# A delta-rule attention and a routed MLP in one kernel: the first inverse moved to one engine, residual and block product in tiles of their own, pairs without padding, late steps routed one by one, and the first 256 places of expert 0 computed between the two stages

## The chip, the cores and the metric

The kernel runs on one core of one Trainium2 chip. The metric is the time of one execution on the device, in microseconds (us). A core has a tensor engine (PE; its weight loads are shown apart, as PEld), a vector engine (DVE), a scalar engine (ACT), a GpSimd engine (POOL) and a sync engine (SP) that issues transfers. Each works through its own queue of instructions in order, and semaphores make one wait for another.

## The reference

Two layers are chained. The first is a linear attention with the delta rule: for each of 4 batches and 8 heads a state of 48 x 48 is carried over 768 tokens. The second is a mixture of 8 experts over the 3072 tokens of width 384, each token going to the one expert with the highest logit.

```python
k_n = k / (np.linalg.norm(k, axis=-1, keepdims=True) + 1e-06)
for t in range(S):
    kt, vt, bt = (k_n[:, :, t], v[:, :, t], beta[:, :, t, None])
    y[:, :, t] = np.einsum('bhd,bhde->bhe', q[:, :, t], state)
    v_old = np.einsum('bhde,bhd->bhe', state, kt)
    state = state + bt[:, :, :, None] * np.einsum('bhd,bhe->bhde', kt, vt - v_old)
...
logits = x @ w_gate
expert_idx = np.argmax(logits, axis=1)
...
for e in range(E):
    h = np.maximum(x_sorted[lo:hi] @ w1[e], 0.0)
    y_sorted[lo:hi] = h @ w2[e]
return (gate_w[:, None] * y).astype(np.float32)
```

With this input the experts get 342 to 410 tokens each, expert 0 gets 401.

## The kernel before, in words

**Chunks and groups.** The 768 tokens are cut into 24 chunks of C = 32; step `c` handles chunk `c` for all 4 batches at once, one batch to each 32 partitions. Inside a chunk the recurrence is a triangular system, one 32 x 32 matrix for each batch and head. Four chunks form a group, `GS = 4`; the inverses of the 128 matrices of a group (4 steps, 8 heads, 4 batches) are made together on DVE by `invert(g)` (L267), one matrix to a partition: transposes in (L281), the norms of the keys by a few operations on 32 columns (L290 to L329), a scaling (L339), 30 pairs of a multiplication (L350) and an addition (L355), one pair to a row of the matrix, a scaling back, and transposes out (L362). The result is `ub`.

**Group 0 is made in another way.** For it `K = 2`: DVE inverts the two 16 x 16 diagonal blocks of each matrix side by side, with 14 pairs instead of 30, and `across` (L376) puts the corner in with matmuls: a product on PE (L384), its eviction on ACT (L389), a second product (L398) and an addition on DVE (L406), once for each of the four steps. These are `chores`, taken at fixed places of the steps.

**A step** (L445). On PE, in this order: the state times the keys is added to the scaled values, which `begin` put there (L439, L453), giving the residual in `pc[:, 0]`; ACT evicts it as `R` (L464); `logits` of an earlier chunk go to columns 384 on of `pc[:, 1]` (L558, evicted at L562); the block product `ub` times `R`, 32 matmuls of 32 x 32 (L473), goes to `pc[:, 1]`, and ACT evicts it as `Z` (L479); the state times the queries (L453); the product of keys and `Z`, added into the sums `acc` (L492), which ACT copies to `states` (L500); the transposes of the chunk before, `turn` (L538), into `pc[:, 0]`; the rest of the output (L511), evicted as `xg` (L521) and written to `xs` in memory. ACT also scales the values of the next chunk (L419). `pc` is one tile of two banks with one buffer, so all these share it.

**What sets the order.** The queues are written out by hand. The main loop (L697) runs a step, lets DVE work on inverses with `fill(4.0)`, runs the small routing work that is `urgent`, computes the scores of a later chunk (`score`, L525, L242), begins the next step, and runs `fill(2.8)`; the argument is a budget in us, which `fill` (L172) charges with 0.165 + 0.00104 n per operation of n elements, or 0.09 + 0.00104 n when it alternates between two inverses. `keep_scores` (L249) masks the scores into `gt` and `qk` with two operations (L260). At the start of a group the loop finishes that group's inverse first. Scores are computed 6 chunks ahead at the start (`FRONT`), and one more at steps 0, 5 and 8 (`EXTRA`). Where no scores are left, `heat` runs a matmul without a use (L431).

**Layouts.** Keys and queries come in pairs of heads: 48 rows of one head padded to 64, so that a pair has 128 rows. `kq` holds them, `wide_kq` holds them again with zeros where the other head is. The keys by token (`kt`) are padded to 64 columns a head.

**Routing** (L568). When the last chunk of a batch of `BATCHES` has its logits, DVE finds each token's expert, PE ranks the tokens of an expert (L605), DVE adds the counts so far (L618 to L631), and POOL writes the tokens' numbers to their places in `lists` by one indirect transfer for each chunk (L633); each waits for the one before. The gates are written beside `xs` (L650). The last batches are chunks 16 to 19, 20 to 22, and 23.

**Experts.** After step 23 (the seam) the lists are read back (L738, L742); for each expert POOL clears a tile and gathers the tokens' rows (L760, L762): three tiles of 128 places and one of 64. `expert` (L775) transposes them, multiplies with w1 (L790), applies the ReLU, multiplies with w2 (L806; the 64 places in another way, L820), scales with the gate and scatters to the output (L770). In fp32 each matmul shows as two entries in the trace. Weights of expert 0 come in pieces during steps 4 to 17; those of experts 1 and 2 are asked for in the seam (L132, L133), when the attention's memory is free.

Of the kernel before, what the change touches and what calls it, by code (L numbers as in the profile page):

```python
# [14 lines left out]
I32 = mybir.dt.int32  # L15
# [6 lines left out]
B, H, S, D = 4, 8, 768, 48  # L22
C = 32
# [17 lines left out]
FRONT = 6  # L41
EXTRA = (0, 5, 8)
LG = DM
RK = LG + E
LEAD = 10
BATCHES = [[0, 1, 2, 3], [4, 5, 6, 7], [8, 9, 10, 11], [12, 13, 14, 15],
           [16, 17, 18, 19], [20, 21, 22], [23]]


def _f32_consts():  # L50

# [11 lines left out]
    own = t // (C // 2) == w // (C // 2)  # L63
    kk = 1.0 * (t == w) - (t < w)
    k0 = 1.0 * (t == w) - ((t < w) & own) - (t // (C // 2) > w // (C // 2))
    return np.concatenate(
        [kk, k0, -1.0 * (t < w), rev, base, more, p < j, np.ones((128, 128))], axis=1
# [4 lines left out]
def kernel(  # L72
# [23 lines left out]
    nc.scalar.dma_start(out=cf[:, 0 : 3 * C], in_=src[:, 0 : 3 * C])  # L96
# [4 lines left out]
    def part(w):  # L101
# [4 lines left out]
    mask_g, mask_0, mask_q, rev, base, further, upper, ones = (  # L106
        part(w) for w in (C, C, C, E, E, E * MAXR, 128, 128)
# [37 lines left out]
    psS = att.enter_context(tc.tile_pool(name="psS", bufs=1, space=PSUM))  # L145
    psC = att.enter_context(tc.tile_pool(name="psC", bufs=1, space=PSUM))
    psQ = att.enter_context(tc.tile_pool(name="psQ", bufs=1, space=PSUM))
    psA = att.enter_context(tc.tile_pool(name="psA", bufs=1, space=PSUM))
    att.enter_context(tc.manual_schedule())
# [3 lines left out]
    states = persist.tile([128, B, NP, 2, D], FP32, name="states")  # L153
    acc = psS.tile([128, B, 512], FP32, name="acc")

    wide_kq = [persist.tile([128, 2, NP, 2, 128], FP32, name=f"wkq{i}") for i in range(3)]
    LW = E * LIST // 128
    empty = persist.tile([128, LW], I32, name="empty")
    warm = persist.tile([128, 512], FP32, name="warm")
    fdt = persist.tile([128, GS * H, C], FP32, name="fdt")  # L160

    kqs, kts, vts, qks, gts, ubs, norms, vss, xgs, lgs = ({} for _ in range(10))
# [3 lines left out]
    behind, later, soon, chores = deque(), deque(), deque(), deque()  # L166
    scored, front = [0], [None]
# [3 lines left out]

    def fill(us):  # L172


        while us > 0 and behind:
            n = next(behind[0], None)
            if n is None:
                behind.popleft()
                continue
            us -= (0.09 if len(behind) > 1 else 0.165) + 0.00104 * n  # L180
            if len(behind) > 1:
                behind[0], behind[1] = behind[1], behind[0]

    def chore():
        if chores:
            chores.popleft()()

    def urgent():

        for work_ in soon:  # L190
            for _ in work_:
                pass
        soon.clear()
        soon.extend(later)
        later.clear()
# [23 lines left out]
    def scores(c):  # L219

        if c >= NS:
            return None
# [697 lines left out]
```

## Time and profile before

| | |
|---|---|
| time, median of 3 runs | 668.01 us (664.99 to 671.21) |
| span of the profiled run | 670.4 us |
| PE, busy | 577.2 us, 86% |
| DVE, busy | 238.6 us, 36% |
| ACT, busy | 169.2 us, 25% |
| POOL, busy | 105.4 us, 16% |
| granted PE clock, mean | 0.923 |
| expert products L790, L806, L820 | 148.5, 125.1, 22.4 us |
| row operations L350 and L355 | 52.7 and 53.0 us |
| heating L431 | 43.8 us, 86 entries |

A line of the profile's groups or timeline gives the engine, the line of the kernel, the operation, output and inputs by name, the shape, and in brackets the idle time of the engine before it and what ended that. `x32` in a timeline is a run of 32 such instructions. Busy PE time is the sum of overlapping entries, so a busy PE need not be PE at its best. A busy share over the whole span mixes stages: the experts fill PE, the steps before them don't. In the strip of 40 slices each digit is a tenth of a slice of 16.8 us; the line PEclk shows the granted clock in tenths.

### The profile page before, as it was taken

Reading aid. Unit: us, or ns where it says so; the run is one execution under the profiler, and the core shown is the slowest. Engines: PE = TensorE matmul, PEld = TensorE weight load, DVE = VectorE, ACT = ScalarE, POOL = GpSimd, SP = SyncE. Lnnn points to the kernel's source line nnn. Section 1 sums busy time; section 2 is a strip of 40 time slices with the busy share of each in tenths; the row PEclk is TensorE's granted clock in tenths of the full one; section 3 lists DMA queues with packets and bytes.
Section 4 is the critical chain, followed back from the end, with each engine's and each line's share of the span. In section 5 each row is a group of like instructions: output and inputs, shape, how many; then the busy total and the mean of one; then the engine's idle time right before and its main releaser. Section 6 shows DMA issues by size and latency. Waiting matters only on the chain. (4 is left out here: it accounts for less than half of the span.)

```text
span 670.4 us, 18338 instructions
## 1 busy us (share of the span) xinstructions
PE 577.2 (86%) x8120; PEld 358.0 (53%) x8121; DVE 238.6 (36%) x773; ACT 169.2 (25%) x441; POOL 105.4 (16%) x111
## 2 busy tenths in 40 slices
PE   4777758847878988887979999999999999999991
PEld 3356646636656765665435555555555545555550
DVE  4825655789967968011111021111102020111100
ACT  0124325434545556552001010101001010101101
POOL 4000000110010101102240131402213140311011
PEclk9967679787989899888989999999999999999996
DMA  9933336655653334211075012423234342310000
GB/s 320 268 103 98 97 96 194 132 144 136 186 143 105 69 93 92 75 37 26 2 247 197 24 51 106 150 95 121 52 123 132 118 142 106 121 33 36 2 23 12
DMA packets 38882, 72.15 MB, mean 108 GB/s; under 512 B 10310, under 2 KB 25078, under 8 KB 38800
## 3 DMA queue, kind: packets, MB, share of 16 engines
q1 hardware_dynamic: 33072, 60.99, 30.7%
q0 software_dynamic: 4608, 9.47, 4.5%
q8 instruction: 64, 1.05, 0.7%
q10 hardware_dynamic: 1120, 0.50, 0.3%
q14 instruction: 18, 0.15, 0.1%
HBM read 62.16 MB, written 10.35 MB: 108 GB/s over the span
## 5 line engine op out<-in xcount | busy, mean ns | idle before, releaser
L790 PE MATMUL phe<-xTe,w1t 128*128 128x448 f32 x384 | 148.5, 547 | 0.0
L806 PE MATMUL pye<-w2t,hT 128*128 128x384 f32 x384 | 125.1, 486 | 0.0
L790 PEld LDWEIGHTS phe<-xTe,w1t 128*128 128x128 f32 x384 | 73.2, 192 | 70.1 <-issue 67.8
L806 PEld LDWEIGHTS pye<-w2t,hT 128*128 128x128 f32 x384 | 73.0, 190 | 51.7 <-issue 3.0
L633 POOL DMA_INDIRECT lists<-ids,ri x24 | 23.5, 979 | 291.7 <-DVE ut L355 140.9
L795 DVE TENSOR_SCALAR hT<-phe 128x448 f32<-128x448 f32 x32 | 20.0, 625 | 127.5 <-PE phe L790 127.5
L770 POOL DMA_INDIRECT out_dram<-y,rows x24 | 24.0, 1002 | 214.5 <-ACT y L815 181.1
L355 DVE TENSOR_TENSOR ut<-ut,tmp 128x58 f32<-128x58 f32 (+9 forms) x164 | 53.0, 323 | 4.8
L350 DVE TENSOR_TENSOR tmp<-ut 128x58 f32<-128x58 f32 (+9 forms) x164 | 52.7, 322 | 5.1
L799 ACT ACTIVATE hT<-phe 128x448 f32<-128x448 f32 x32 | 17.4, 543 | 144.6 <-PE phe L790 144.6
L419 ACT ACTIVATE vs<-vt,normt 128x48 f32<-128x48 f32 x192 | 47.8, 324 | 7.8 <-DVE normt L324 7.8
L473 PE MATMUL pc<-R,ub 32*32 32x48 f32 x1472 | 25.1, 222 | 24.0 <-DVE tmp L350 10.1
L500 ACT ACTIVATE states<-acc 48x768 f32<-48x768 f32 x46 | 37.0, 804 | 32.8 <-PE acc L492 28.7
L431 PE MATMUL pa<-warm,ident 128*128 128x512 f32 x86 | 43.8, 655 | 0.0
L785 DVE COPY xTe<-px 128x448 f32<-128x448 f32 x24 | 14.2, 614 | 80.7 <-PE px L781 80.7
L815 ACT ACTIVATE y<-pye,xin 128x384 f32<-128x384 f32 x16 | 9.3, 580 | 133.2 <-PE pye L806 133.2
L492 PE MATMUL acc<-Z,kt 32*128 32x96 f32 x736 | 33.3, 324 | 3.3 <-issue 3.3
L473 PEld LDWEIGHTS pc<-R,ub 32*32 32x32 f32 x1472 | 21.2, 119 | 26.9 <-issue 19.2
L558 PE MATMUL pc<-wg,xT 128*128 128x8 f32 x144 | 21.3, 268 | 13.9 <-ACT R L464 10.3
L492 PEld LDWEIGHTS acc<-Z,kt 32*128 32x128 f32 x736 | 28.8, 227 | 8.4 <-issue 6.1
L811 DVE TENSOR_SCALAR y<-pye,xin 128x384 f32<-128x384 f32 x8 | 4.9, 618 | 78.0 <-PE pye L806 78.0
L558 PEld LDWEIGHTS pc<-wg,xT 128*128 128x128 f32 x144 | 19.1, 202 | 18.6 <-ACT R L464 13.6
(109 smaller groups left out, 574.0 us busy)
## 6 DMA issues: line engine op xcount, KB each, us to landing
kq<-in_kq_t_dram SPq DMA_DIRECT2D x24, 512.0 KB
w1t<-in_moe_w_dram SPq DMA_DIRECT2D x7, 1536.0 KB
w2t<-in_moe_w_dram SPq DMA_DIRECT2D x7, 1536.0 KB
kt<-in_k_tok_dram SPq DMA_DIRECT2D x24, 256.0 KB
wkq<-in_kq_t_dram SPq DMA_DIRECT2D x30, 192.0 KB
vt<-in_v_tok_dram SPq DMA_DIRECT2D x24, 192.0 KB
xs<-xg SPq DMA_DIRECT2D x24, 192.0 KB
wkq<-in_kq_t_dram SPq DMA_DIRECT2D x6, 256.0 KB
```

The lines of the kernel that those rows point to most:

```text
L350: nc.vector.tensor_tensor(out=tv, in0=ud[:, :, j + 1 : W, j].unsqueeze(3).to_broadcast([128, K, n, j]), in1=ud[:, :, j, 0:j].unsqueeze(2). ...
L355: nc.vector.tensor_tensor(out=ud[:, :, j + 1 : W, 0:j], in0=ud[:, :, j + 1 : W, 0:j], in1=tv, op=OP.add)
L419: nc.scalar.activation(out=vss[c][:, h, :], in_=vts[c][:, h, :], func=AF.Copy, scale=norms[g][:, H * s + h : H * s + h + 1],)
L431: nc.tensor.matmul(pa[:], lhsT=ident[:], rhs=warm[:], start=True, stop=True, skip_group_check=True)
L473: nc.tensor.matmul(pc[rows_of(b), 1, D * h : D * h + D], lhsT=ub[rows_of(b), H * s + h, :], rhs=R[rows_of(b), h, :], start=(h == 0), stop= ...
L492: nc.tensor.matmul(acc[:, b, 96 * p : 96 * p + 96], lhsT=kt[rows_of(b), p, :], rhs=Z[rows_of(b), 2 * p : 2 * p + 2, :], start=(c == 0 and ...
L500: nc.scalar.activation(out=states[r, :, :, e], func=AF.Copy, scale=-1.0, in_=acc[r, :, 0:DM].rearrange("q b (p e w) -> q b p e w", p=NP, e ...
L558: nc.tensor.matmul(pt[:, LG : LG + E], lhsT=xT[:, s, :], rhs=wg[:, s, :], start=(s == 0), stop=(s == NK - 1), skip_group_check=True,)
L633: nc.gpsimd.indirect_dma_start(out=lists, out_offset=bass.IndirectOffsetOnAxis(ap=ri[:, i : i + 1], axis=0), in_=ids[:, ss[i] : ss[i] + 1] ...
L770: nc.gpsimd.indirect_dma_start(out=out, out_offset=bass.IndirectOffsetOnAxis(ap=index, axis=0), in_=y[0:w, :], in_offset=None, bounds_chec ...
L790: nc.tensor.matmul(ph[:], lhsT=w1t[:, s, f * 128 : f * 128 + 128], rhs=xT[:, s, :], start=(s == 0), stop=(s == NK - 1),)
L806: nc.tensor.matmul(py[:], lhsT=hT[:, f, t * 128 : t * 128 + w], rhs=w2t[:, f, :], start=(f == 0), stop=(f == NF - 1),)
```

## The change

It has seven parts that belong together.

1. **First inverse on DVE.** Group 0 is inverted like the others; `across`, `chores`, the second mask and `fdt` go. To bridge the longer inverse, the scores of 8 chunks (`FRONT = 8`) are computed ahead, from `wide_kq` into the four banks of `acc`, whose first loads wait for the clearing of that tile; heating is split into 6 and 12 matmuls. One extra score remains, at step 5.
2. **Own tiles.** `pc` becomes `pv` (residual, and `turn`) and `pz` (block product, logits, ranks).
3. **Block product in pairs.** ACT spreads `ub` of two batches into a block diagonal of 64 x 64 (`spread_out`, two copies for a group), and the product takes 16 matmuls of 64 x 64 instead of 32 of 32 x 32.
4. **Unpadded pairs.** 96 rows instead of 128 for `kq`, `wide_kq`, `states`, `acc`; `kt` without padding; the sums are copied to `states` with a per-row factor of 0 or -1, which clears the other head's half.
5. **One mask.** `gt` and `qk` become one tile `km`, written by one operation of 512 elements.
6. **Late steps routed singly.** From chunk 16 on every chunk is a batch; from step 16 (`LATE`) `turn` runs in the step before the block product, in the tile `pa`, and the logits follow the queries' product.
7. **Expert 0's first 256 places in the seam.** After chunk 19 is listed (`CLOSED`), the count of expert 0 is raised to at least 256, and `first_places` gathers the first 256 places at the end of step 21, transposes them at the end of step 22, and multiplies with w1 and w2 from step 23 on, between the last routing work; `heat(24)` becomes `heat(4)`. Expert 0 then has one tile of 128 and one of 64 places left. Places are cut into tiles anew for it.

`fill` now spends its budget on the first inverse alone unless that one is well ahead of its group, and the second budget of a step is 3.2 instead of 2.8.

```diff
-FRONT = 6
-EXTRA = (0, 5, 8)
+EARLY = 2
+CLOSED = 19
+FRONT = 8
+EXTRA = (5,)
-LEAD = 10
+LEAD = 9
+LATE = 16
-           [16, 17, 18, 19], [20, 21, 22], [23]]
+           [16], [17], [18], [19], [20], [21], [22], [23]]
...
+            two = len(behind) > 1 and 1.8 * first_[2] < 7.0 * left - 4.0
+            for each in list(behind)[: 1 + two]:
...
+                            pa[rows_of(b), 128 * p + 64 * e : 128 * p + 64 * e + 64],
+                            lhsT=wide[:, e, p, 0, rows_of(b)], rhs=wide[:, e, p, :, rows_of(b)],
...
-        K = 1 if g else 2
...
-        for j in range(W - 2, 0, -1):
-            n = W - 1 - j
+        for j in range(C - 2, 0, -1):
+            n = C - 1 - j
...
+    def spread_out(steps=(0, GS)):
+        g, ub = spread[0]
+        if g not in ubs:
+            ubs[g] = block.tile([128, GS * H, 2, C], FP32, name="ubw")
+        a, b = (H * s for s in steps)
+        for k in range(2):
+            nc.scalar.activation(
+                out=ubs[g][:, a:b, k], in_=ub[:, a:b], func=AF.Copy, scale=own[:, k : k + 1]
+            )
...
+        if c >= LATE:
+            turn(c - 1)
...
-            for b in range(B):
+            for r in two_of:
                 nc.tensor.matmul(
-                    pc[rows_of(b), 1, D * h : D * h + D], lhsT=ub[rows_of(b), H * s + h, :],
-                    rhs=R[rows_of(b), h, :], start=(h == 0), stop=True, skip_group_check=True,
-                )
-        chore()
+                    pz[r, D * h : D * h + D],
+                    lhsT=ub[r, H * s + h].rearrange("q k w -> q (k w)"),
+                    rhs=R[r, h, :], start=(h == 0), stop=True, skip_group_check=True,
+                )
...
-                out=states[r, :, :, e], func=AF.Copy, scale=-1.0,
+                out=states[:, :, :, e], func=AF.Copy, scale=mine[0:DD, e : e + 1],
...
+        if c == CLOSED + 2:
+            early.append(first_places(*weights[0]))
+            ahead_of_time(1)
...
-        fill(2.8)
+        if c == NS - 2:
+            ahead_of_time(1)
+        fill(3.2)
...
-    turn(NS - 1, psA.tile([128, 512], FP32, name="pa", tag="pa"))
     logits()
-    soon.reverse()
-    while soon or later or counted:
-        urgent()
-        logits()
-    heat(24)
+    ahead_of_time(1)
+    turn(NS - 1)
+    ahead_of_time(1)
+    urgent()
+    while soon or later or counted or turned:
+        logits()
+        ahead_of_time(2)
+        urgent()
+    ahead_of_time(99)
+    heat(4)
     att.close()
```

`first_places` (shortened):

```diff
+        xin = block.tile([128, EARLY, ROW], FP32, name="exin", tag="ub")
+        nc.gpsimd.memset(xin[:], 0.0)
+        nc.gpsimd.dma_start(
+            out=index[:], in_=lists[0:W, :].rearrange("(p t) o -> p (t o)", t=EARLY)
+        )
...
+        for f in range(NF):
+            ph = psE.tile([128, W], FP32, name="eph")
+            for s in range(NK):
+                nc.tensor.matmul(
+                    ph[:], lhsT=w1t[:, s, f * 128 : f * 128 + 128], rhs=xT[:, s, :],
+                    start=(s == 0), stop=(s == NK - 1),
+                )
...
+        for t in range(EARLY):
...
+            put(index[:, t : t + 1], y, 128)
+            yield 1
```

## The prediction

> **What bounds the kernel now.** I read the page's strip of 40 slices first, then the busy time by stage, then the timeline around the two longest idle times of the tensor engine, one ordinary step, and the seam between attention and experts.
>
> ```profile
> PE   4777758847878988887979999999999999999991
> DVE  4825655789967968011111021111102020111100
> PEclk9967679787989899888989999999999999999996
> ```
>
> A slice is 16.8 us. From slice 21 on PE is full: the experts are matmul time. Before that neither PE nor DVE is full and the granted clock dips, so work is handed to and fro.
>
> ```profile
> core 0: us, PE busy (x) PEld busy (x) DVE busy (x) ACT busy (x) POOL busy (x), PEclk, DMA share, GB/s
> 0.00:34.10 34.10, 19.17 (x532) 11.39 (x533) 22.90 (x75) 4.38 (x15) 7.38 (x15) 1.00 0.96 293
> 34.10:99.97 65.87, 47.17 (x1511) 36.86 (x1515) 33.14 (x103) 21.86 (x61) 0.00 (x0) 0.71 0.33 98
> 99.97:155.49 55.52, 38.23 (x1108) 30.16 (x1111) 40.40 (x153) 22.06 (x63) 4.06 (x4) 0.84 0.56 142
> 155.49:306.50 151.01, 129.22 (x3743) 96.40 (x3741) 94.54 (x334) 81.85 (x228) 14.58 (x15) 0.93 0.41 105
> 306.50:348.10 41.60, 35.00 (x254) 19.13 (x254) 6.53 (x39) 3.58 (x12) 15.52 (x15) 0.88 0.25 71
> 348.10:387.00 38.90, 38.90 (x116) 20.41 (x115) 3.75 (x6) 3.66 (x7) 3.02 (x3) 0.95 0.38 138
> 387.00:659.80 272.80, 269.56 (x866) 143.61 (x865) 37.37 (x64) 31.83 (x58) 60.87 (x59) 1.00 0.26 87
> ```
>
> The stages are: prologue up to the first block product; to Z of step 4; to Z of step 8; to R of step 23; seam; expert 0; experts 1 to 7. Steps 0 to 7 take 121 us, 15 each, though DVE works 74 of them; the later ones about 10 each.
>
> ```profile
> 98.41 1.50 PE L473 MATMUL pc<-R,ub 32*32 32x48 f32 x64 [7.28 <-DVE ub L362]
> 153.93 1.50 PE L473 MATMUL pc<-R,ub 32*32 32x48 f32 x64 [10.08 <-DVE tmp L350]
> ```
>
> At steps 4 and 8 PE stands 7.3 and 10.1 us until the group's inverse is ready (by then the clock is down: these 64 take 1.50, elsewhere 0.88).
>
> ```profile
> 206.53 0.49 ACT L464 ACTIVATE R<-pc 128x384 f32<-128x384 f32 x1 [1.45 <-PE pc L453]
> 207.07 0.83 PE L558 MATMUL pc<-wg,xT 128*128 128x8 f32 x6 [0.61 <-ACT R L464]
> 207.95 0.18 ACT L562 ACTIVATE lg<-pc 128x8 f32<-128x8 f32 x1 [0.93 <-PE pc L558]
> 208.18 0.88 PE L473 MATMUL pc<-R,ub 32*32 32x48 f32 x64 [0.27 <-ACT lg L562]
> ```
>
> In an ordinary step the logits wait for R's eviction, and the block product for theirs, since all share the tile pc.
>
> ```profile
> 329.36 0.97 POOL L633 DMA_INDIRECT lists<-ids,ri  x1 [2.42 <-DMA lists<-ids,ri]
> 336.50 1.04 POOL L762 DMA_INDIRECT xin<-xs,rows  x1 [6.17 <-DMA rows<-lists]
> 340.46 0.96 POOL L762 DMA_INDIRECT xin<-xs,rowh  x1 [0.30 <-issue]
> 345.55 2.63 PE L781 MATMUL px<-ident,xin 64*128 64x64 f32 x9 [2.88 <-DMA xin<-xs,rowh]
> 348.11 1.11 PE L790 MATMUL phe<-xTe,w1t 128*128 128x448 f32 x1
> ```
>
> The seam is a chain: last list write, lists read back, four gathers, transposes. PE is busy there only with 48 heating entries (22.4 us).
>
> **What the skill says.** "TensorE: Matmul & The Clock Gate", on the HAM clock gate, has PE fall to half rate after an idle window of about 3.4 us; the trace agrees (granted 0.71 to step 4, full where PE is dense). "TensorEngine Tiling (Array Packing)", Available Configurations, gives four tiles at 64x64 against sixteen at 32x32; the trace shows only the latter for block products. "VectorE: DVE Perf Modes", on the TRN2 errata, prices an fp32 tensor_tensor at (N+151)/0.96 ns: 0.407 us at 240, 0.424 at 256; the trace has 0.41 and 0.42. "DMA: Bandwidth & Descriptors", Anatomy of one DMA, gives a GpSimd DMA about 2 us of fixed time; the list writes wait 2.0 to 2.6 for the one before, beyond 0.97 of issue.
>
> **The change part by part.**
>
> *Prologue.* One inverse on DVE, from the rows of the trace: transposes in 2.1 us, the norm 3.6, scalings 2.1, the 60 row operations 19.8 busy (9.9 each for L350 and L355) plus 60 gaps of 0.035, transposes out 1.9: about 31.8. Group 0 now runs it whole. Scores come from the zero-padded loads, sent only when the memsets end (about 2 us instead of 0.8), so start near 5, at 1.2 to 1.4 a piece; with one mask (512 elements, 0.69 by the price above) the fourth is masked at 11.2. Adding 31.8 and two more masks (1.4), and two short ACT copies: the first block product at 45 instead of 34.1, +11. DMA (0.96 busy there) gets less: 96 rows instead of 128, no 64-padding.
>
> *Steps 0 to 3.* The correction of group 0 goes: 256 + 256 entries on PE (6.7 us), four m copies, four adds whose waits stood in DVE's queue (14.2 us). The scores of steps 4 to 7 are done ahead, so DVE goes straight on to inverse 1: 45 + 1.4 + 31.8 + four masks 2.8 + waits gives 83, the spread on ACT (two copies of 1024; 768 take 0.80, so 1.05 each) 85. PE needs about 10 a step, cold at first, as before: 45 + 41 = 86. I take Z of step 4 at 88 against 99.97. This turns +11 into -12.
>
> *Steps 4 to 19.* Per group of four DVE owes 31.8 + four masks 2.8 + routing 3.8 (route 1.2, listed 2.0, gates 0.6) = 38.4. PE's step at full clock was 8.5; residual and block product in own tiles save the 0.61 and shorten the way to the block product by 0.6 in all; the product falls from 64 to 32 entries, two tiles at a time: between half (0.44) and all (0.88) of its time, I take 0.66; the state product has 96 weight columns for 128 (0.98 to about 0.87). Some 7.6 to 8, plus the clock dips that raised 8.5 to 10 on average. Against this ACT makes two spreads of 1.05 per group ahead of R, some 2 us each fourth step. So DVE sets the group, a little above 38.4: 40 to step 8, 40 to 12, 39 to 16, 39 to 20. Z: 128, 168, 207, 246; before 155.5, 199.3, 240.3, 278.3.
>
> *Steps 20 to 23.* Routing singly adds about 2.6 of DVE per step, where DVE is idle, and 0.6 of PE; an own tile for the turn frees the residual's. Z20 to R23 took 28.2; I take 27: R23 at 273 for 306.5, -33.5.
>
> *Seam.* Three list writes of about 3.3 leave the chain, but POOL now issues both early puts ahead of xin's memset, and the second waits for the end of the early product. From xg23 (R23 + 7): 48 entries of 256 columns at 0.215 (0.43 for 512, halved) 10.3, 32 of 384 at 0.326 10.4, other PE work and cold clock 4: 24.7. Eviction 0.6, put 1.0, memsets 0.7 and 1.4, gathers 1.3 and 1.0: 30.7. From its issue to its transposes a last gather took 5.1 (340.46 to 345.55), bounded below by the 4.0 of the first: 34.5 to 35.8; then 2.0: 36.2 after xg23, where it took 34.6 before. The seam is as long as before (43.2 for 41.6), only filled.
>
> *Expert 0.* 192 places: 48 entries at 192 x 0.375/448 = 0.16 (the floor is a weight load, 0.74 for the six of L558, 0.12 each), 7.9; one full tile 5.2, half tile 2.8, the next expert's transposes 2.3, and about 1.8 for a cold start: 20 instead of 38.9. Expert 1's weights, 3.1 MB at the 220 GB/s that slices 20 and 21 of the strip moved (247 and 197), need 14 us from the landing of the puts; 27 are there.
>
> Sum: -33.5 + 1.6 - 18.9 = -50.8; from 668 I forecast **618**.
>
> **The rivals.**
> *DVE does not bind* (two inverses interleave; PE runs at 9.0 from step 4): R23 at 86 + 19 x 9.0 = 257, 16 sooner: 602. For it: 8.5 us steps exist. Against: PE's stops without a releaser (1.9 us at 187.6) and DVE 80% busy already.
> *The hand-overs cost more*: spreads ahead of R and clock dips keep groups at 43 (steps 8 to 12 took 43.9), prologue +3, fetch +3: 618 + 12 + 6 = 636. For it: every inverse ends just at its boundary in DVE's new order.
> *Slower*: steps stay at 11.85 each (306.5 - 34.1 over 23), so R23 at 45 + 272 = 317, the seam takes 43, and expert 1's weights, freed only after the puts, hold it until 39 later: 399 for 387, so 680. Against: it needs none of the removed waits to have mattered.
>
> **How the numbers follow.** Forecast 0.54, fast rival 0.2, costly hand-overs 0.2, slower 0.06. The range 602 to 640 reaches both middle rivals and holds the unknowns (block product 0.44 to 0.88, 23 steps: 10 us; gather latency: 1; prologue: 3). Faster by over 1% 0.92, same 0.03, slower 0.05.
>
> **What would show it.** First block product near 45; no stop over 3 us at steps 4 and 8; Z20 near 246; 0.16 per entry in expert 0; the gather after the second put; no wait on w1t. A stage PE cannot fill, or expert 1 waiting for weights, would make it wrong.

## The result, and the profile after

The changed kernel takes 634.72 us (median of 4 runs, 626.45 to 640.97) where the kernel before took 666.50 in the same comparison. The ratio is 0.951, with a 95% interval of 0.937 to 0.965: faster. The forecast was 618 with a range of 602 to 640, so the direction and the range held and the point was 17 us too low. A ratio leaves out the slowest runs (over 1.5% above the fastest of their kernel), so it need not be the quotient of the medians. Single runs of one kernel lie up to 2.3% apart, so most of what follows is read from stages of profiles and not from totals.

The strip of the changed kernel, 40 slices of 15.8 us:

```profile
PE   4694979889889989979949999999999999999990
DVE  3699997979898886212100201111011110201100
```

PE is denser from slice 4 on than before, DVE is full in slices 2 to 5 (the first two inverses), and the hole at the end of the attention is slice 20, at 316 to 332 us. Its busy time by stage, with the same columns and the same cuts as before (first block product; Z of step 4; Z of step 8; R of step 23; first product of expert 0; expert 1; end of the products):

```profile
core 0: us, PE busy (x) PEld busy (x) DVE busy (x) ACT busy (x) POOL busy (x), PEclk, DMA share, GB/s
0.00:54.33 54.33, 31.58 (x548) 19.93 (x549) 36.81 (x102) 4.16 (x13) 4.91 (x12) 0.96 0.86 195
54.33:92.98 38.65, 32.49 (x935) 26.32 (x939) 35.67 (x113) 25.59 (x66) 0.00 (x0) 0.90 0.50 136
92.98:135.02 42.04, 37.10 (x980) 29.46 (x984) 35.37 (x120) 23.91 (x64) 3.06 (x3) 0.87 0.75 169
135.02:279.75 144.73, 129.97 (x3290) 101.05 (x3290) 105.47 (x395) 87.61 (x243) 21.74 (x22) 0.89 0.47 102
279.75:329.19 49.44, 39.94 (x253) 29.15 (x253) 7.54 (x47) 6.37 (x18) 12.93 (x13) 0.78 0.23 75
329.19:349.13 19.94, 19.90 (x93) 15.06 (x92) 3.15 (x8) 2.64 (x7) 1.04 (x1) 0.90 0.54 211
349.13:621.20 272.07, 267.87 (x857) 142.53 (x856) 36.00 (x62) 31.47 (x57) 60.73 (x59) 1.00 0.26 87
```

Beside the forecast, in us (a group is four steps, measured from Z to Z):

| stage | before | forecast | after |
|---|---|---|---|
| to the first block product | 34.1 | 45 | 54.3 |
| steps 0 to 3 | 65.9 | 43 | 38.7 |
| steps 4 to 7 | 55.5 | 40 | 42.0 |
| steps 8 to 11 | 43.9 | 40 | 39.7 |
| steps 12 to 15 | 41.0 | 39 | 38.1 |
| steps 16 to 19 | 38.0 | 39 | 39.3 |
| Z of step 20 to R of step 23 | 28.2 | 27 | 27.7 |
| seam | 41.6 | 43.2 | 49.4 |
| expert 0 | 38.9 | 20 | 19.9 |
| from expert 1 on | 272.8 | 272.8 | 272.1 |

These two profiled runs lie 38.6 us apart at the end of the products; the medians lie 31.8 apart. The gain comes mostly from steps 0 to 7 and from expert 0. The prologue and the seam give 28 us of it back, 15.5 more than forecast.

The stops at steps 4 and 8, which were 7.3 and 10.1 us, in the timeline of the changed kernel (start, duration, engine and line, what; in brackets the idle time before it and what ended that):

```profile
88.31 2.19 ACT L442 ACTIVATE ubw<-ub,cf 128x1024 f32<-128x1024 f32 x2 [2.87 <-DVE ub L429]
91.00 1.94 PE L513 MATMUL pz<-R,ubw 64*64 64x48 f32 x32 [3.39 <-ACT lg L608]
...
130.35 2.19 ACT L442 ACTIVATE ubw<-ub,cf 128x1024 f32<-128x1024 f32 x2 [3.65 <-DVE ub L429]
133.03 1.94 PE L513 MATMUL pz<-R,ubw 64*64 64x48 f32 x32 [0.45 <-ACT lg L608]
```

At step 4 PE still waits 3.39 for ACT, and ACT had waited 2.87 for the inverse and then made the two spreads ahead of R and of the logits. At step 8 ACT waits again (3.65), but PE is late itself and hardly does. The clock records of the trace are either full or half; they are half from 90.8 to 97.6 us and from 128.3 to 138.5. There the 32 entries take 1.94 us, which the text below calls half rate.

What shortened steps 4 to 7 can be read on DVE. The first two lines are from the kernel before, the third from the changed one:

```profile
105.60 0.42 DVE L260 TENSOR_TENSOR gt<-pa,cf 128x256 f32<-128x256 f32 x1 [7.34 <-PE pa L242]
...
141.76 0.63 DVE L281 STREAM_TRANSPOSE ut<-gt 128x256 f32<-128x256 f32 x1
...
88.13 2.03 DVE L351 STREAM_TRANSPOSE ut<-km 128x256 f32<-128x256 f32 x4
```

Before, DVE was done with the inverse of group 1 at 98.3 us and then idled 7.34 for scores that PE makes only in step 4, and PE had itself just waited for that inverse. The inverse of group 2 ran from 106.3 to 153.8, and at 141.8 DVE took up group 3 beside it. In the changed kernel the scores are there: DVE goes on to group 2 at 88.1 without a gap, is done at 130.3, and takes up group 3 only at 127.4.

In an ordinary step at full rate the 32 entries take 1.13:

```profile
202.46 0.83 PE L604 MATMUL pz<-wg,xT 128*128 128x8 f32 x6
202.60 0.49 ACT L504 ACTIVATE R<-pv 128x384 f32<-128x384 f32 x1 [2.27 <-PE pv L493]
203.33 0.18 ACT L608 ACTIVATE lg<-pz 128x8 f32<-128x8 f32 x1 [0.24 <-PE pz L604]
203.56 1.13 PE L513 MATMUL pz<-R,ubw 64*64 64x48 f32 x32 [0.27 <-ACT lg L608]
```

The logits now run on PE while ACT evicts R: the wait of 0.61 is gone, the one of 0.27 is left. The seam:

```profile
304.84 0.97 POOL L684 DMA_INDIRECT lists<-ids,ri  x1 [9.04 <-DVE su L698]
305.48 10.48 PE L228 MATMUL epy<-w2t,ehT 128*128 128x384 f32 x32
308.04 0.34 SPq L802 DMA_DIRECT2D rows<-lists  x1
...
311.74 0.97 POOL L173 DMA_INDIRECT out_dram<-ey,eindex  x1 [5.93 <-ACT ey L233]
316.86 0.97 POOL L173 DMA_INDIRECT out_dram<-ey,eindex  x1 [4.14 <-ACT ey L233]
...
320.07 1.05 POOL L830 DMA_INDIRECT xin<-xs,rows  x1 [0.16 <-POOL xin L828]
321.42 0.96 POOL L830 DMA_INDIRECT xin<-xs,rowh  x1 [0.30 <-issue]
...
326.93 1.06 PE L843 MATMUL px<-ident,xin 128*128 128x128 f32 x4 [7.54 <-issue]
```

The lists were asked for at 308.0, but POOL stands in its queue before the second put, which waits for the early product, and only then clears the tile and gathers. PE idles 7.54 us.

### The profile page after: what moved, and what is told of

Its sections match the earlier page's. It is cut to its first block, busy times and chain, and to the rows that moved or that the text cites. A ratio compares the mean times of both kernels' runs of the same rounds, so it can differ in the third digit from the quotient of the medians.

```text
span 632.0 us, 16133 instructions
## 1 busy us (share of the span) xinstructions
PE 558.9 (88%) x6944; PEld 363.5 (58%) x6945; DVE 260.0 (41%) x844; ACT 181.8 (29%) x466; POOL 104.4 (17%) x110
## 5 line engine op out<-in xcount | busy, mean ns | idle before, releaser
L852 PE MATMUL phe<-xTe,w1t 128*128 128x448 f32 (+1 forms) x384 | 138.1, 521 | 0.0
L422 DVE TENSOR_TENSOR ut<-ut,tmp 128x30 f32<-128x30 f32 (+9 forms) x180 | 59.7, 332 | 5.9
L417 DVE TENSOR_TENSOR tmp<-ut 128x30 f32<-128x30 f32 (+9 forms) x180 | 59.2, 329 | 5.8
L542 ACT ACTIVATE states<-acc,cf 96x768 f32<-96x768 f32 x46 | 38.7, 891 | 15.7 <-PE acc L534 13.8
L513 PE MATMUL pz<-R,ubw 64*64 64x48 f32 x736 | 30.7, 241 | 9.6 <-ACT lg L608 8.4
L513 PEld LDWEIGHTS pz<-R,ubw 64*64 64x64 f32 x736 | 27.6, 156 | 12.9 <-ACT lg L608 9.9
L552 PE MATMUL pq<-Z,km 32*32 32x48 f32 x1536 | 26.1, 219 | 3.8 <-issue 3.8
L468 PE MATMUL pa<-ident 128*128 128x512 f32 x58 | 29.0, 638 | 0.0
L311 PE MATMUL acc<-wkq 96*32 96x64 f32 x512 | 15.1, 290 | 14.9 <-DMA wkq<-in_kq_t_dram 12.3
L552 PEld LDWEIGHTS pq<-Z,km 32*32 32x32 f32 x1536 | 21.8, 118 | 8.6 <-issue 8.0
L534 PE MATMUL acc<-Z,kt 32*96 32x96 f32 x736 | 25.5, 285 | 0.6 <-ACT Z L519 0.6
```

The costliest lines, as they stand in the source:

```text
L417: nc.vector.tensor_tensor(out=tv, in0=full[:, j + 1 : C, j].unsqueeze(2).to_broadcast([128, n, j]), in1=full[:, j, 0:j].unsqueeze(1).to_br ...
L422: nc.vector.tensor_tensor(out=full[:, j + 1 : C, 0:j], in0=full[:, j + 1 : C, 0:j], in1=tv, op=OP.add)
L468: nc.tensor.matmul(out, lhsT=ident[:], rhs=ident[:].unsqueeze(1).to_broadcast([128, out.shape[1] // 128, 128]), start=True, stop=True, ski ...
L513: nc.tensor.matmul(pz[r, D * h : D * h + D], lhsT=ub[r, H * s + h].rearrange("q k w -> q (k w)"), rhs=R[r, h, :], start=(h == 0), stop=Tru ...
L534: nc.tensor.matmul(acc[0:DD, b, DD * p : DD * p + DD], lhsT=kt[rows_of(b), 2 * p : 2 * p + 2, :], rhs=Z[rows_of(b), 2 * p : 2 * p + 2, :], ...
L542: nc.scalar.activation(out=states[:, :, :, e], func=AF.Copy, scale=mine[0:DD, e : e + 1], in_=acc[0:DD, :, 0:DM].rearrange("q b (p e w) -> ...
```

## The experiments

The 12 kernels are compared by ratio with the kernel before, run on the same chip (the changed kernel's ratio is 0.951), and by the stages of one profile each. The runs lie on more than one chip, so medians of different kernels are not set side by side.

### The prologue: tiles of the scores, and the masks in the inverse

The prologue of the changed kernel:

```profile
7.01 1.95 PE L311 MATMUL acc<-wkq 96*32 96x64 f32 x62 [0.65 <-DMA wkq<-in_kq_t_dram]
...
12.65 2.06 PE L311 MATMUL acc<-wkq 96*32 96x64 f32 x64 [0.84 <-DVE km L335]
...
17.63 0.69 DVE L335 TENSOR_TENSOR km<-acc,cf 128x512 f32<-128x512 f32 x1 [2.13 <-PE acc L311]
18.36 2.13 DVE L351 STREAM_TRANSPOSE ut<-km 128x256 f32<-128x256 f32 x4
...
25.98 1.95 PE L311 MATMUL acc<-wkq 96*32 96x64 f32 x62 [0.61 <-DMA wkq<-in_kq_t_dram]
...
28.04 1.29 DVE L335 TENSOR_TENSOR km<-acc,cf 128x512 f32<-128x512 f32 x2 [2.04 <-PE acc L311]
```

A piece of scores takes 1.95, not 1.2 to 1.4, and the third and fourth wait for the mask of the piece before, though they go to another bank. In the middle of the inverse DVE waits 2.04 for the scores of chunk 5, and these wait for their load. The first run gives the four pieces tiles of their own.

```diff
-            pa = acc[:, c % B, :]
+            pa = (
+                acc[:, c % B, :] if c in (0, 4, 5, 6, 7)
+                else (psA, psQ, psC)[c - 1].tile([128, 512], FP32, name=("pa", "pq", "pv")[c - 1])[:]
+            )
```

> The changed kernel with the first four scores in four PSUM tiles (acc, pa, pq, pv) instead of four banks of the one tile acc. Theory: a score waits for the mask of the one before only because they share a tile; without that the fourth mask comes at about 14 instead of 17.6, the first inverse starts 3.5 us sooner, the first block product falls from 54.3 to about 50.8, Z4 from 93.0 to 89.5, and since DVE sets the groups the gain stays to the end: total about 3.5 us less (631). Rivals: the loads of the third and fourth chunk bind, and the inverse starts less than 1 us sooner; or the gain is made but gone by Z8, because PE and ACT set the groups.

The inverse began at 16.2 instead of 18.4, but the first block product came at 53.3 and Z4 at 92.5, 1.1 and 0.5 sooner. The wait in the middle had grown from 2.04 to 3.19: half of what was won ahead of the inverse was lost in it. The pieces no longer wait for masks, and still take about 1.95. Ratio 0.943 (0.933 to 0.953). In this profile the granted clock of steps 8 to 11 was 0.76, and it is not read further. Loads do bind, as the rival had it, but those of chunks 4 and 5 more than those that it named: the inverse did start 2.2 us sooner. So the second run takes the masks of chunks 4 and 5 out of the inverse too.

```diff
         if c == GS:
             fill(8.0)
-            for a in ahead:
-                keep_scores(*a)
+            first_ahead = ahead
...
-    for a in ahead:
+    for a in first_ahead + ahead:
         keep_scores(*a)
```

> As the run with four score tiles, and the masks of chunks 4 and 5 come after the first inverse instead of in its middle, where DVE waited 2.0 us (3.2 in that run) for their scores, which wait for their loads. Theory: the loads feed the prologue; what remains on DVE is the fourth mask at 15.5, the inverse from 16.2 without a stop, and the first block product at 49.5 to 50 instead of 54.3; Z4 at 88.5 to 89 instead of 93.0. Rival: the inverse is held by something else too, or Z4 is set by PE's cold steps 0 to 3: first product above 52, or Z4 above 91.5.

```profile
13.20 1.15 PE L314 MATMUL pv<-wkq 96*32 96x64 f32 x62 [0.20 <-DMA wkq<-in_kq_t_dram]
14.41 0.69 DVE L338 TENSOR_TENSOR km<-pv,cf 128x512 f32<-128x512 f32 x1 [2.03 <-PE pv L314]
15.14 2.07 DVE L354 STREAM_TRANSPOSE ut<-km 128x256 f32<-128x256 f32 x4
...
47.90 1.13 PE L516 MATMUL pz<-vs,ubw 64*64 64x48 f32 x32 [0.80 <-ACT ubw L445]
```

The first block product came at 47.9, 6.4 sooner, Z4 at 87.8 (5.2 sooner), Z20 at 246.3 (5.8 sooner): the lead was kept through all groups. The last two pieces took 1.13 and 1.15, at full rate, where the run before this one, with the same tiles, had 1.98 and 1.95. So about 1 us of the 6.4 is a rate that the edit didn't set and that need not come again; it came in one more of the runs below. The rest is 2.2 by which the tiles let the inverse begin sooner, the 2.04 for which it no longer waits, and 1.3 for the two masks that now come behind it. Ratio 0.946 (0.939 to 0.954), whose interval overlaps that of the changed kernel; the stages carry the finding.

### The gather between steps 22 and 23

The last step took 13.9 us from R22 to R23, its neighbour 8.0. The timeline of the changed kernel there:

```profile
273.38 0.30 PE L200 MATMUL pa<-ident,exin 128*128 128x128 f32 x1 [2.32 <-DMA exin<-xs,eindex]
...
275.64 0.90 PE L200 MATMUL pa<-ident,exin 128*128 128x128 f32 x3 [1.96 <-DMA exin<-xs,eindex]
...
278.18 1.51 PE L493 MATMUL pv<-states,kq 96*32 96x96 f32 x32
```

PE's queue holds the transposes of the early rows ahead of step 23, waits 4.3 us for the rows, and then does step 23 at half rate (1.51 where 0.87 is usual). In the run below the places are closed one chunk sooner.

```diff
-CLOSED = 19
+CLOSED = 18
```

> The changed kernel with expert 0's early places closed after chunk 18 instead of 19, so that the index and the early rows are asked for one step (7 to 8 us) sooner. Theory: PE's wait of 2.3 and 2.0 us for the early rows between steps 22 and 23, and the half clock after it, cost the 5.5 us by which the last step is longer than its neighbours; R23 comes near 274.3 instead of 279.8, and all that follows moves with it: total about 5.5 us less (629). Rival: the clock falls there anyway, or the seam has a fixed end (list chain, POOL) that takes the time back: total less by under 2 us.

```profile
280.77 0.66 PE L200 MATMUL pa<-ident,exin 128*128 128x128 f32 x4
```

From R22 to R23 it took 8.9 instead of 13.9, with the transposes unwaited for and the products of step 23 at full rate. The other profiles agree: this step takes 10.2 to 14.9 us in all seven that close after chunk 19, and 7.9 to 8.9 in the three that close after chunk 18. The theory holds for the step. That profile had one group of 45.8 us (steps 8 to 11, clock 0.80), so its R23 lies at 283.5 in spite of it. Ratio 0.935 (0.926 to 0.944), some 10 us below the changed kernel's with intervals that overlap; so much is not this wait alone.

### The seam: fetch first, and no early places at all

```diff
+    def fetch_rest():
+        nc.sync.dma_start(
+            out=rest0[:], in_=byexp[0, EARLY * 128 : ST * 128].rearrange("(p t) -> p t", t=ST - EARLY)
+        )
...
+        for t, (index, n) in enumerate(((rest0[:, 0:1], 128), (resth[:, 0:1], HALF))):
+            nc.gpsimd.indirect_dma_start(
+                out=xin0[0:n, t, :], out_offset=None, in_=xs,
...
+    fetch_rest()
     ahead_of_time(99)
...
-    xin = fetch(mlp, places[0])
+    xin = xin0
```

> The changed kernel with the two remaining tiles of expert 0 read back and gathered ahead of the two early puts on POOL, into a tile of their own that is cleared at the start (for its room the scratch of the inverse has 3 buffers instead of 4). Theory: the second put, which waits for the end of the early product, gates the gathers. Then the gathers are issued at about 311 and 312 instead of 320.1 and 321.4, land near 317, and the first product of expert 0 comes after the heating at 321 to 322 instead of 329.2: total about 7.5 us less (627). Rival: PE is not free and the last list write lands too late for more; the first product moves by at most 3 us. In neither does anything before 305 us change.

```profile
306.06 1.04 POOL L154 DMA_INDIRECT xin<-xs,rest  x1 [4.87 <-DMA rest<-lists]
...
312.24 0.99 POOL L191 DMA_INDIRECT out_dram<-ey,eindex  x1 [2.55 <-ACT ey L251]
...
314.61 1.61 PE L862 MATMUL px<-ident,xin 128*128 128x128 f32 x6
...
316.15 2.06 PE L871 MATMUL phe<-xTe,w1t 128*128 128x192 f32 x11
```

From the last xg to the first product of expert 0 it took 30.5 us instead of 41.1, and expert 1 started at 334.2 instead of 349.1. Of these 14.9 us, 2.4 lie in a shorter last step and 1.9 in expert 0 itself (18.0 instead of 19.9); of the 10.6 in the seam 2.2 are a quicker list chain (last list write 14.6 after xg, not 16.8), and some 8 are the edit's, near the 7.5 expected. So the second put did gate the gathers. Ratio 0.941 (0.933 to 0.950), whose interval overlaps that of the changed kernel.

```diff
-            early.append(first_places(*weights[0]))
-            ahead_of_time(1)
...
-    heat(4)
+    heat(24)
```

> The changed kernel without part 7: no early places, expert 0 whole (448 places) after the seam, 24 heating matmuls as before. Nothing of the computation is left out. Theory: part 7 is worth little beyond part 6. Without it PE has no gather to wait for at step 22 to 23 (5.5 us), so R23 falls from 279.8 to about 274.3; with the late chunks routed singly only one list write is left after the last xg, so the first product of expert 0 comes about 28 us after xg23 (about 310.5) instead of 41.1; expert 0 then takes 38.9 instead of 19.9, and expert 1 starts at about 349.5 as in the changed kernel (349.1): total 635, within 3 us. Rival, the accounting of the prediction: the seam without early work is as long as before the change (41.6 from R23), first product at 316, expert 1 at 355: total 6 us longer. Second rival: the early part is worth nearly all of its 18.9 us: total 647 or more.

R23 came at 274.4, as the theory had it, and the last list write at 286.1, 6.8 after the last xg. But the first product came at 320.8 and expert 1 at 362.1, 13 us later than in the changed kernel; ratio 0.975 (0.966 to 0.983). The queues of SP and POOL show why:

```profile
289.63 0.39 SPq L136 DMA_DIRECT2D w1t<-in_moe_w_dram  x1
...
296.49 5.68 SPq L801 DMA_DIRECT2D rows<-lists  x1
...
311.14 1.04 POOL L829 DMA_INDIRECT xin<-xs,rows  x1 [24.12 <-DMA rowh<-lists]
```

Here the weights of experts 1 and 2 stand ahead of the lists; in the kernel before (332.6 and 340.8) and in the changed kernel (308.0 and 319.6) the lists go first. The lists then wait behind 6 MB, and the gathers begin at 311.1. The total lies where the second rival had it (0.975 of 666.5 is 650), but not for its reason, so this run does not tell what part 7 is worth with the order of the lists kept. It does show that lists behind weights hold the seam.

### Parts alone

The kernel before with only the own tiles of part 2:

```diff
-        front[0] = psC.tile([128, 2, 512], FP32, name="pc")
+        pv = psC.tile([128, 512], FP32, name="pv") if c else None
+        front[0] = pv, psC.tile([128, 512], FP32, name="pz")
```

> The kernel before with part 2 alone: residual and block product in tiles of their own. Theory: this part is off the path, because DVE (inverses, and in group 0 the corrections) sets the groups: total 0 to 5 us less than before (about 664 of 667). Rival, the saving per step that the prediction counted (0.6 us of hand-over in each of 23 steps): about 14 us less.

Ratio 0.979 (0.968 to 0.991), 14 us: the total of the rival. But it did not come as 0.6 a step. Steps 0 to 3 took 61.0 (before 65.9), 4 to 7 54.9 (55.5), 8 to 11 43.7 (43.9), 12 to 15 37.9 (41.0), 16 to 19 37.3 (38.0), Z20 to R23 23.4 (28.2). In steps 4 to 11, where PE stood waiting for inverses before, nothing was saved; in the last steps, where DVE has next to nothing to do, 4.8 in a little over three steps.

```diff
-        K = 1 if g else 2
+        K = 1
...
-            (gts[g][:, H * s : H * s + H, :], pa[:, :, :, 0], mask_g if g else mask_0),
+            (gts[g][:, H * s : H * s + H, :], pa[:, :, :, 0], mask_g),
```

> The kernel before with the core of part 1 alone: the first inverse whole on DVE, no corrections by matmul; all else, FRONT = 6 too, stays. Theory: the first block product moves from 34.1 to about 47 (31.8 of inverse and 1 of waits after the fourth mask), but Z4 comes sooner than before (about 93 instead of 100) because no adds stand in DVE's queue, and Z8 at 143 instead of 155; later groups keep the lead: total 8 to 12 us less. Rival: without the scores made ahead and the new share of fill's budget the lead is gone by Z8 or the second inverse is late: total within 3 us of before.

First product at 46.7 and Z4 at 92.1, as expected; 7.8 of lead at Z4, 7.2 at Z8, 5.8 at Z20. In the runs the ratio is 0.996 (0.991 to 1.000), some 3 us, less than in the profile. So the stage was right and the sum is within the rival's bound; in steps 4 to 7 this kernel needs 56.2 as before, and so does the kernel with the own tiles alone (54.9), so what brought those to 42 is in the rest of the change (one inverse first, more scores ahead, one mask) or in parts together. In both kernels DVE still idles after the inverse of group 1 until the scores come, 6.54 and 6.83 us, as the kernel before did (7.34); in the changed kernel this gap is gone. So the scores ahead are the likeliest part, but none was tried singly.

```diff
-            for r in two_of:
+            for r in map(rows_of, range(B)):
                 nc.tensor.matmul(
                     pz[r, D * h : D * h + D],
-                    lhsT=ub[r, H * s + h].rearrange("q k w -> q (k w)"),
+                    lhsT=ub[r, H * s + h, :],
```

The spreads are left out with it.

> The changed kernel with part 3 undone: the block product takes 32 matmuls of 32x32 from ub directly, and ACT makes no spreads. Theory: the pairs cost time: their 32 entries take 1.14 us in the changed kernel's trace against 0.88 for 64 entries of 32x32 before, and the two spreads of 1.1 stand ahead of R at each group. Since DVE sets the groups, most of this is hidden in the middle: first block product 0.9 sooner, Z20 4 to 5 us sooner, steps 20 to 23 1 us shorter: total 5 to 6 us less. Rival A: each group gains its 2.2 us and four times 0.26: 3.2 per group, 16 or more in all. Rival B, the prediction's: the pairs save 0.2 a step, so undoing them costs 5 us at the end.

The 64 small entries took 0.88 at full rate, as before the change. Z4 came 3.6 sooner, steps 20 to R23 took 26.5 instead of 27.7, but two groups took 44 to 46 us at a clock of 0.79 and 0.81, and R23 came 2.6 later. Ratio 0.947 (0.938 to 0.957): not distinguishable from the changed kernel. Inconclusive for the size, and the pairs bring no gain that can be seen.

### What sets a group

This run leaves 16 of the 30 row pairs of the inverses of groups 1 to 5 out, so its output is not that of the reference:

```diff
         for j in range(C - 2, 0, -1):
+            if g and 8 <= j < 24:
+                continue
```

> The changed kernel with 16 of the 30 row pairs of the inverses of groups 1 to 5 left out (rows 8 to 23; the result then differs from the reference, the experts' token counts stay within 5 of theirs): 13 us less DVE work in a group. Theory: DVE sets the groups, so each falls from about 40 to what PE and ACT need, 33 to 36, Z20 comes at about 225 instead of 252, total 22 to 30 us less. Rival: PE and ACT with their hand-overs need the 39 to 40 themselves; groups stay above 38 and the total falls by under 8 us.

```profile
core 0: us, PE busy (x) PEld busy (x) DVE busy (x) ACT busy (x) POOL busy (x), PEclk, DMA share, GB/s
88.92:124.15 35.23, 32.65 (x981) 25.90 (x983) 29.34 (x112) 23.72 (x64) 2.26 (x2) 1.00 0.74 188
124.15:167.86 43.71, 38.58 (x947) 30.75 (x945) 22.39 (x82) 24.06 (x65) 5.97 (x6) 0.80 0.76 158
167.86:205.00 37.14, 33.92 (x937) 25.81 (x939) 22.63 (x84) 24.23 (x66) 3.10 (x3) 0.95 0.48 101
205.00:241.00 36.00, 32.27 (x844) 24.52 (x838) 14.96 (x79) 24.29 (x72) 5.82 (x6) 1.00 0.43 81
```

Each line is a group, the column before the last two is the granted clock. At a clock of 1.00 a group takes 35 to 36, and neither PE nor ACT waits for an inverse at a boundary any more: that is what PE and ACT need. One group fell to 0.80 and took 43.7. Z20 came at 241.0 instead of 252.1, ratio 0.928 (0.915 to 0.941), some 15 us less: between the 22 to 30 of the theory and the under 8 of the rival. The four groups changed by -6.8, +4.0, -1.0 and -3.3. So neither expectation held as put. In the changed kernel ACT waits for the inverse ahead of four of the five boundaries (2.87, 3.65, 1.81, none, 1.35 us), so DVE sets most of its groups; but PE and ACT, at full rate, need only some 4 us less than its mean of 39.8, and where the rate drops they need more.

The second question was whether the stops of PE that have no releaser come from transfers.

```diff
-        if c == GS:
+        if c == 3 * GS:
             weights[0] = start_w(wpool)
...
-        if pieces:
+        for _ in range(min(2, len(pieces))):
             pieces.popleft()()
```

> The changed kernel with expert 0's weights asked for in steps 12 to 18, two pieces a step, instead of steps 4 to 17. Theory: PE's stops without a releaser lie at multiples of about 127 matmul entries (with their weight loads about 254 instructions), whatever the instruction, so they are waits for instructions to arrive, and transfers of weights lengthen them; each is followed by some 6 us at half clock. Then between Z4 and Z12 the stops (4.0 us in the changed kernel) fall below 1.5 us, the clock rises from 0.87 to above 0.93 and both groups come down to 36 to 38 from 42.0 and 39.7; groups 12 to 20 get slower by as much, the total stays within 1%. Rival: the stops don't depend on the transfers; groups 4 to 12 stay at 39 to 43 and the clock at 0.85 to 0.9.

Between Z4 and Z12 one stop above 0.35 us was left, of 2.5, where there were four, of 4.0 together; but the clock was 0.82 and 0.84, and the groups took 42.6 and 39.9, as in the changed kernel (42.0 and 39.7). Ratio 0.959 (0.952 to 0.965), within 1% as both expected. For the time of the groups the rival holds. That the stops got fewer did not show in them.

### All together

Four edits in one kernel: fetch first, closing after chunk 18, score tiles with the masks after the inverse, and `heat(1)` for `heat(4)` in the seam.

```diff
+    fetch_rest()
...
-CLOSED = 19
+CLOSED = 18
...
-    heat(4)
+    heat(1)
```

> The changed kernel with four things together: the rest of expert 0 gathered ahead of the early puts, early places closed after chunk 18, four score tiles with the masks of 4 and 5 after the inverse, and one heating matmul instead of four in the seam. Theory: the four waits lie one after the other on one path, so the gains add: 7 to 10, 5, 4 and 2 us: total 612 to 618. Rival: a gain in the prologue or at step 23 is taken back by PE and its clock in the groups: total 620 to 625.

607.63 us (605.38 to 611.65, 6 runs), ratio 0.924 (0.919 to 0.928), which lies wholly below the interval of the changed kernel. First product 47.6 (54.3), Z20 246.2 (252.1), R23 271.0 (279.8), first product of expert 0 302.6 (329.2), expert 1 320.6 (349.1). Nothing was taken back: 28.5 us less in the profile at expert 1, of which 17.8 lie in the seam, 6.8 in the prologue and 2.9 from Z20 to R23; about 18 by the ratios of the runs (0.924 of 666.5 is 616, inside the theory's 612 to 618). In the groups of this profile PE has no stop without a releaser above 0.35 us, and yet they took 41.2, 39.9, 37.4 and 40.2; the waits of PE between Z4 and Z20 (us in total, times, longest):

```profile
PE pz L534 <- ACT lg L629: 10.2, 12, 3.5
...
123.98 2.19 ACT L463 ACTIVATE ubw<-ub,cf 128x1024 f32<-128x1024 f32 x2 [3.07 <-DVE ub L450]
```

PE comes early to the group's boundary and stands there. ACT had waited for the inverse (3.07 at step 8, then 2.19 of spreads) before it evicted R and the logits, and it waits so ahead of all five boundaries (5.63, 3.07, 1.53, 2.25, 1.36). So the group's length stays what DVE makes it.

The last run adds the small blocks of the run above to this one.

> As the run with the four things together, and the block product of 32x32 from ub without spreads. Theory: the pairs cost 0.26 us a step and 2.2 us ahead of R at each group on the path of PE and ACT; PE sets the groups where the clock is down, so 3 to 6 us less than without this. Rival: 32 more matmul entries a step bring more stops of PE at every 127 entries, which takes the gain back: within 2 us of it, or slower.

608.08 us, ratio 0.922 (0.918 to 0.927): the rival, within 2 us. The 32 entries more a step did come with stops, 13 above 0.3 us and 15.5 us together from the first block product to R23, where the run with the four edits had none:

```profile
161.18 0.45 PE L573 MATMUL pq<-Z,km 32*32 32x48 f32 x21 [1.48 <-issue]
...
171.36 0.78 PE L573 MATMUL pq<-Z,km 32*32 32x48 f32 x34 [2.16 <-issue]
```

Between these two lie 254 matmul entries. At no group's boundary does PE or ACT wait for an inverse here, and yet the four groups take 164 us together, against 159 in the run before: PE and ACT, with PE's stops, are the limit now. The gain of the blocks and the loss by the stops were not separated.

## Why the prediction was right, and where it was off

The range held and the sum came within 17 us. A part of the errors cancels: the prologue and the seam were put 15.5 us too short, and steps 0 to 3 4.3 too long. (The prediction's own sum gives 617.2, which it put down as 618.)

- **Prologue: mis-sized, +9.3.** The step "start near 5, at 1.2 to 1.4 a piece; the fourth is masked at 11.2" failed. The fourth mask was done at 18.3. The first piece started at 6.0; the pieces took 1.95 to 2.06 at half rate; one wait of 0.65 was for a load, and before each of the next three pieces PE stood 0.84 to 0.89, for the third and fourth behind the mask of the one before, because the four banks are one tile. Another 2.0 was the wait for the scores of chunk 5 and their load, placed in the middle of the inverse. The inverse itself was right: in the run without that wait it took from 15.1 to 46.9, the 31.8 of the forecast.
- **Steps 0 to 3: 38.7 for 43.** The forecast had two chains here, DVE's inverse with ACT's spread (45 to 85, so 40) and PE's 41, and took PE's as the limit. ACT waits 2.87 for the inverse at 88.3, so DVE's was the limit, and PE needed less than was put down. This returned half of the prologue's loss.
- **DVE sets the groups: right, but close.** All four groups were within 2.1 us of the forecast. With 13 us less of DVE work in each, Z20 came 11 sooner, not 50 or more, because PE and ACT need 35 to 36 at the best clock. The block product was outside both bounds (1.13 at full rate, not 0.44 to 0.88), and this cost nothing that the runs can tell, as the forecast had DVE ahead.
- **Steps 20 to 23: the number right by luck.** 27.7 for 27. PE and ACT without a wait need 22.3 for this stretch (the run without early places), and the wait for the early rows with the half rate after it added 5.0 to 5.5. The prediction named no such wait, though part 7 puts the transposes into PE's queue ahead of step 23.
- **The seam: mechanism right, terms too small.** "POOL now issues both early puts ahead of xin's memset, and the second waits for the end of the early product" is what the trace shows, and the run with the fetch ahead of the puts takes some 8 us away. Of the 6.2 us that were missing, 1.3 lie ahead of the last xg (it was done 8.3 after R23, where 7 was put down), 3.5 from there to the second put (28.8 for 25.3) and 1.4 after it (12.3 for 10.9). The early products with w1 took 17.2 us, with routing between them, where 10.3 and a share of 4 were put down; part of step 23 and of this ran at half rate. From the issue of the last gather to its own transposes it took 6.1 (321.4 to 327.5), where 4.0 to 5.1 had been taken. The prediction's own terms also add up to 36.5 to 37.8 after the last xg, where it went on with 36.2. (Its waits of 2.0 to 2.6 between list writes are those of the last three; earlier ones waited 1.7 to 5.7.)
- **Expert 0: right**, 19.9 for 20, with 0.163 us an entry at full rate for the 0.16 forecast, and expert 1 had no wait for its weights. The run with the fetch ahead of the puts, where expert 0 starts at full rate, has 18.0, so the 1.8 for a cold start was right too.
- **The signs.** Right were the gather after the second put, the 0.16 an entry and no wait on w1t. Missed were the first block product (54.3 for 45), Z20 (252.1 for 246) and, by a little, no stop over 3 us at steps 4 and 8 (3.39 at step 4).
- **The rival of costly hand-overs** gave 636, nearest to the result, but not by its own terms: groups of 43 did not come (42.0, 39.7, 38.1, 39.3), its 3 us in the prologue were 9.3, and its 3 us in the fetch 6.2.
- **Own tiles** bring 14 us alone, the total that the prediction's 0.6 a step would give without DVE ahead, but not step by step: 4.9 in steps 0 to 3, 4.8 in the last three, and next to nothing in steps 4 to 11.

## What to carry to other kernels

Where two engines need nearly the same time for a stage, a forecast from the slower one can be exact and still say little: here 13 us less on DVE in each of five groups brought 11 in all. Look at what stands in an in-order queue behind a wait that an added part brings with it: the four edits gave 28 us in the profile and some 18 in the runs, and three of them only move work in a queue (a gather ahead of a put, rows one step ahead of their use, two masks behind the inverse). Banks still waited for each other here, 0.84 to 0.85 us a piece, as long as the program called them one tile. And where two engines wait for each other in turn, as DVE for scores and PE for the inverse in steps 4 to 7, work made ahead for one frees both.

## What was not expected of the hardware

- **Blocks of 64x64 are slower here than twice as many of 32x32.** 32 entries of 64x64x48 in fp32 take 1.13 us at full rate, 64 entries of 32x32x48 take 0.88: 35 against 14 ns an entry, so half the entries cost more time.
- **PE stops while its instructions arrive.** In several traces PE idles 0.4 to 4 us with no releaser, whatever the instruction, mostly at places whose distances are multiples of 127 to 128 matmul entries (seven of the eight stops above 0.3 us in the attention of the changed kernel). An entry has a weight load, so 127 are 254 instructions. The page lists an instruction queue whose sizes fit:

```profile
q8 instruction: 55, 0.90, 0.7%
```

  0.90 MB in 55 packets is 16 KB a packet, and PE's 13,889 entries and weight loads make 253 to a packet. In the traces of six of the kernels, 47 of the 58 such stops above 0.3 us end 1.2 to 1.7 us after the end of one of these packets, though the packets come 5 to 6 us apart, so that chance would give about one in twelve. So most of these stops are waits for instructions; the other 11 are not explained. Why one trace has none and another 13 stays open, and moving the weights' transfers did not settle it. The Trainium skill, "Runtime: NRT & Kernel Launch", Instruction fetch mechanics, has blocks of 16 KiB or 256 instructions and calls the cost mostly hidden. The size agrees; mostly hidden holds only in part, as seven such stops take 6.7 us of the attention of the changed kernel, and twelve take 14.8 in the last run.
- **The granted clock reads full where nothing was recorded.** Pieces of 1.95 us, which take 1.13 to 1.15 at full rate, stand in a stage whose granted clock reads 0.96. The trace of the changed kernel has no clock record before 29.3 us, and a stretch without one counts as full: 0 to 29.3 us reads 1.00. So this number says nothing on the prologue. In the run with the masks behind the inverse the records begin at 10.4 us, with the full clock, just where its pieces get faster.
